# Attention with a transformed, normalised channel mixing on one core: where exponentials, first conversions and mixing steps are issued

## The chip, the cores and the metric

One core of a Trainium2 chip. The metric is the device time of one execution in microseconds (us), here the median of three runs. TensorE does the matrix products, VectorE, ScalarE and GpSimd (POOL in the rows) the elementwise work, and SyncE (SP) issues most DMA transfers. Every engine works through its own instructions in the order in which the program issues them to it.

## The reference

There are 4 batches of 8 heads; the sequence is 1152 long, a head 64 wide. Queries are averaged in pairs, so 576 remain.

```python
q_pool = q.reshape(B, H, S // 2, 2, D).mean(axis=3)
scores = np.matmul(q_pool, k.transpose(0, 1, 3, 2)) / np.sqrt(D)
attn = np.exp(scores - np.max(scores, axis=-1, keepdims=True))
attn = attn / (np.sum(attn, axis=-1, keepdims=True) + 1e-09)
x = merge_heads(np.matmul(attn, v))                      # (4, 576, 512)
u = x + np.real(np.fft.fft(np.fft.fft(x, axis=1), axis=2))
un = (u - mean(u)) / np.sqrt(var(u) + 1e-06)
out = u + np.maximum(un @ w_ch1, 0.0) @ w_ch2            # 512 -> 2048 -> 512
```

The weights `w_ch1` and `w_ch2` are in double precision.

## The kernel before

**Attention** goes over 16 pairs of heads (four per batch) and five units per pair. Units 0 to 3 hold 128 queries of each of the two heads (two tiles), unit 4 the last 64 of both (one tile). The generator `attention()` (line 290) writes out the order of the work by hand, and each `yield` hands the planner the TensorE time, in ns, of what it has just issued. In unit i these stand in turn: two score pieces of the next unit (`some(2)`), the value product of the unit before (`finish`, `av`, line 241: 36 matmuls, and a ScalarE copy, line 252), transposes of the first four key chunks (`tr`, `t_step`, line 225) with their copy from PSUM to SBUF (line 235), two score pieces, the second transposes, the exponentials of tiles that have all their three pieces (`exps()`), two score pieces, the last three groups of transposes (the second of them copied by VectorE), and the exponentials that are left.

A score piece (`s_piece`, line 197) is two matmuls of 384 keys and a VectorE eviction that keeps the running minimum (line 210). An exponential (`s_exp`, line 216) is one ScalarE operation over the tile's 1152 keys, with a read of its sum.

**PSUM** has eight tiles of one bank: five in `ps_t`, for score pieces and, from pair 4 on, for transposes; one for value products; two in `ps_f`, for transposes of pairs 0 to 3, for the transforms and the mixing. While attention goes on, the mixing uses the two of `ps_f` only.

**Heads.** Two float32r parts, high and low, stand in for one float32 factor. For heads 0 and 1 the loads come in pieces, and `k_part` and `q_part` (lines 153 to 165) convert them on ScalarE and VectorE, each piece right before the score piece that needs it; head 1's pieces follow head 0's exponential (lines 304 to 310). The loads of head 2 wait for the last exponential issued so far (`later`, line 136). Later heads are loaded in units 0 and 2 of the pair before and converted in units 1 and 3, on GpSimd and ScalarE.

**Weights.** `convert(f, which)` (line 531) turns one block of 512 KB of doubles into two float32r parts: a load (buffer `wraw`, two of them), three ScalarE operations (540, 546, 555), four VectorE operations (542 to 551), three GpSimd operations (556 to 558), a store to DRAM (561). The buffers between are single. There are 32 blocks.

**Transforms and norm.** After the last pair of a batch, `mid(b)` (line 663) issues the Fourier products and the normalisation in some fifty steps, each with its TensorE time and a due time for the next one; many of these are `gap`, 1300 ns (lines 405 and 469), 0 in the last batch.

**Channel mixing.** `ffn(b)` (line 597) has 64 steps of 12 matmuls, planned at 1600 ns each. For a step of the first product, ScalarE takes the relu from PSUM (line 611) and VectorE the low part (line 612). In batch 0 a block waits in the plan until the one two places on has been converted and stored (line 639).

**The planner** (lines 671 to 751) keeps a clock `now`, in ns of TensorE work issued, and a `credit`. After each `yield` of attention:

```python
now += pe
credit = min(credit + pe * RATE, 4000.0)
if now >= cdue and todo and len(busy) < 2:
    converter()
    cdue = now + 9000
```

It then issues what is due: a transform step where its due time has come, else mixing steps while `credit` is over 0; both are taken off `credit`. Ahead of pairs 10, 12 and 14 (`finish`, line 385) the attention outputs need a buffer of an earlier batch, and `drain` issues mixing steps, whatever the credit, until that batch is through (60 of 64 steps of batch 0, all of it, 60 of batch 1). What is left after attention is the tail.

Of the kernel before, what the change touches and what calls it, by code (L numbers as in the profile page):

```python
# [20 lines left out]
B, H, S, D = 4, 8, 1152, 64  # L21
# [25 lines left out]
def fused_kernel(ctx: ExitStack, tc: tile.TileContext, k2, q2, v2, w1, w2, cst, out):  # L47
    nc = tc.nc
    pool = lambda name, bufs, **kw: ctx.enter_context(tc.tile_pool(name=name, bufs=bufs, **kw))
    ctx.enter_context(tc.manual_schedule())  # L50
    RATE = 0.88
    XB = 5
# [163 lines left out]
    def s_exp(n, j):  # L216
        pr = n // 2
        if pr not in den:
# [4 lines left out]
                                           accum_out=den[pr][:, col:col + 1]).ins  # L223

    def t_step(pr, items, eng):

        if pr < 4:
            ps = ps_f.tile([P, 512], F32, tag="f", name="f")
        else:
            ps = ps_t.tile([P, 512], F32, tag="t", name="t")  # L230
# [59 lines left out]
    def attention():  # L290
# [12 lines left out]
        units = [(pr, j) for pr in range(NP) for j in range(5)]  # L303
        for n, (_, q_part, _, k_part, _) in enumerate(first):
            for pc in range(3):
                k_part(*K0[pc])
                if pc == 0:
                    q_part(*Q0[0])
                s_piece(n, 0, pc)
            s_exp(n, 0)  # L310
        nc.sync.dma_start(onesm, cst[4, :, P:2 * P])
# [5 lines left out]
        for i, (pr, j) in enumerate(units):  # L317
# [40 lines left out]
            if j < 4:  # L358
                a, b = tiles
# [12 lines left out]
            yield tr(g[1], "a")  # L372
            exps()
            yield some(2)
# [23 lines left out]
    def dft(b):  # L398
# [5 lines left out]
        last = smp.tile([1, SQ], F32, tag="last", name="last", bufs=1)  # L404
        gap = 1300 if b < B - 1 else 0
        nc.vector.tensor_copy(tmp[D:D + 1], ub[:1])
# [60 lines left out]
    def norm(b):  # L467
        ua, ub = ut[b]
        gap = 1300 if b < B - 1 else 0
        sm = mtile([P, 2, SQ], F32, "lsum")  # L470
# [57 lines left out]

    wsc = {}

    def convert(f, which):
        src = (w1, w2)[which]
        w = cvp.tile([P, 512, 2], I32, tag="wraw", name="wraw", bufs=2)
        nc.sync.dma_start(w, src[f].bitcast(I32).rearrange("p (c x) -> p c x", x=2))
        yield 6000
        high, low = w[:, :, 1], w[:, :, 0]
        t = cvp.tile([P, 2, 512], F32, tag="wt", name="wt")
# [19 lines left out]
        nc.gpsimd.tensor_tensor(t[:, 1, :], t[:, 1, :], hi.bitcast(F32), op=ALU.subtract)  # L557
        nc.gpsimd.tensor_tensor(lo.bitcast(F32R), t[:, 1, :], rest, op=ALU.add)  # L558
        yield 4000
        d = scw.tile([P, 2, 512], F32, name=f"w{which}_{f}")  # L560
# [110 lines left out]
    now = due = credit = 0.0  # L671
    cdue = 24000.0
    events = []
# [63 lines left out]
    for pe in attention():  # L737
        now += pe
        credit = min(credit + pe * RATE, 4000.0)
        if now >= cdue and todo and len(busy) < 2:  # L740
            converter()
            cdue = now + 9000
        run_events()
# [69 lines left out]
```

## Time and profile before

| | us |
|---|---|
| median of 3 runs | 1145.65 |
| lowest, highest | 1144.2, 1150.67 |
| the profiled execution, its own time | 1142.13 |
| its span, first to last instruction | 1140.4 |
| TensorE, VectorE, ScalarE, GpSimd busy in it | 1038.2, 603.5, 524.8, 361.9 |
| mean granted TensorE clock, share of 2.4 GHz | 0.961 |

Times in the rows count from the start of the span. Matmuls are pipelined, so the durations of single ones overlap, and the busy time of a group of them says less than the starts of one and the next.

### The profile page before, as it was taken

Reading aid. Unit: us, or ns where it says so; the run is one execution under the profiler, and the core shown is the slowest. Engines: PE = TensorE matmul, PEld = TensorE weight load, DVE = VectorE, ACT = ScalarE, POOL = GpSimd, SP = SyncE. Lnnn points to the kernel's source line nnn. Section 1 sums busy time; section 2 is a strip of 40 time slices with the busy share of each in tenths; the row PEclk is TensorE's granted clock in tenths of the full one; section 3 lists DMA queues with packets and bytes.
Section 4 is the critical chain, followed back from the end, with each engine's and each line's share of the span. In section 5 each row is a group of like instructions: output and inputs, shape, how many; then the busy total and the mean of one; then the engine's idle time right before and its main releaser. Section 6 shows DMA issues by size and latency. Waiting matters only on the chain.

```text
span 1140.4 us, 21940 instructions
## 1 busy us (share of the span) xinstructions
PE 1038.2 (91%) x8688; PEld 947.2 (83%) x8688; DVE 603.5 (53%) x1550; ACT 524.8 (46%) x1045; POOL 361.9 (32%) x343
## 2 busy tenths in 40 slices
PE   4888887897899898999999999999999899998998
PEld 2777776776788897799988998899989879998998
DVE  4476575867666557664463455744265244242222
ACT  3676675655765454564453445545156212121111
POOL 0446565675464544643222223222020010000000
PEclk9998898898899898989999999999999999998999
DMA  5644554633465756264534443335520423544554
GB/s 155 191 134 154 168 160 155 209 124 111 148 217 170 240 193 223 75 207 135 178 108 148 139 147 98 92 119 163 184 70 22 151 74 104 163 153 158 167 167 152
DMA packets 53708, 168.96 MB, mean 148 GB/s; under 512 B 8083, under 2 KB 11300, under 8 KB 53606
## 3 DMA queue, kind: packets, MB, share of 16 engines
q1 hardware_dynamic: 49286, 149.87, 41.1%
q0 software_dynamic: 4320, 17.70, 5.0%
q8 instruction: 68, 1.11, 0.4%
q14 instruction: 34, 0.28, 0.1%
HBM read 145.97 MB, written 21.57 MB: 147 GB/s over the span
## 4 chain that ended last, share of the span: by engine, by line
PE 68%; DVE 9%; POOL 6%; ACT 5%; DMA 5%; issue 5%; SPq 1%; POOLq 0%; DVEq 0%; ACTq 0%
PE o L248 12%; PE s L208 9%; PE f L593 7%; PE f L595 7%; PE f L594 7%; PE t L232 6%; PE t L593 4%; PE t L595 4%; PE t L594 4%; DVE sp L210 4%; DMA w<-wraw 2%; POOL wraw L558 2%; POOL wt L557 2%; PE f L232 2%; DMA w<-w 1%
## 5 line engine op out<-in xcount | busy, mean ns | idle before, releaser
L210 DVE TENSOR_SCALAR_CACHE_REDUCE sp<-s,bia 128x384 f32<-128x384 f32 x288 | 177.2, 615 | 87.7 <-PE s L208 67.8
L208 PE MATMUL s<-ks,qh 128*128 128x384 f32 x480 | 189.3, 394 | 37.4 <-ACT qh L156 11.4
L222 ACT ACTIVATE sp<-sp,bia 128x1152 f32<-128x1152 f32 x144 | 181.7, 1261 | 23.2 <-DVE sp L210 22.9
L248 PE MATMUL o<-pt,vs 128*64 128x128 f32 (+1 forms) x2880 | 182.2, 280 | 8.3 <-ACT pt L235 7.0
L248 PEld LDWEIGHTS o<-pt,vs 128*64 128x64 f32 x2880 | 160.1, 146 | 33.9 <-issue 21.0
L208 PE MATMUL s<-ks,ql 128*128 128x384 f32 x480 | 166.9, 348 | 0.0
L235 ACT COPY pt<-t 128x512 f32<-128x512 f32 (+2 forms) x228 | 116.3, 522 | 75.9 <-PE t L232 74.1
L232 PE MATMUL t<-ident,sp 128*128 128x128 f32 x972 | 141.4, 279 | 3.6 <-DVE sp L210 3.3
L208 PEld LDWEIGHTS s<-ks,qh 128*128 128x128 f32 x480 | 94.1, 196 | 49.2 <-DVE sp L210 14.9
L232 PEld LDWEIGHTS t<-ident,sp 128*128 128x128 f32 x972 | 116.8, 143 | 14.8 <-DVE sp L210 5.4
L593 PE MATMUL f<-unh,w 128*128 128x288 f32 x332 | 102.3, 308 | 5.5 <-DMA w<-w 5.5
L593 PE MATMUL f<-g,w 128*128 128x288 f32 x336 | 103.1, 307 | 1.6 <-DMA w<-w 1.6
L612 DVE SCALAR_TENSOR_TENSOR g<-f,g 128x288 fp32r<-128x288 f32 x83 | 38.0, 457 | 117.5 <-ACT g L611 117.5
L595 PE MATMUL f<-g,w 128*128 128x288 f32 x336 | 99.5, 296 | 0.0
L594 PE MATMUL f<-g,w 128*128 128x288 f32 x336 | 99.4, 296 | 0.0
L594 PE MATMUL f<-unh,w 128*128 128x288 f32 x332 | 99.1, 298 | 0.0
L595 PE MATMUL f<-unl,w 128*128 128x288 f32 x332 | 98.8, 298 | 0.0
L208 PEld LDWEIGHTS s<-ks,ql 128*128 128x128 f32 x480 | 94.9, 198 | 0.7 <-DVE ql L157 0.3
L623 DVE TENSOR_TENSOR x<-f,x 128x288 f32<-128x288 f32 x84 | 38.4, 457 | 103.8 <-PE f L595 103.7
L556 POOL TENSOR_TENSOR rest<-rest,wt 128x512 f32<-128x512 f32 x32 | 43.6, 1361 | 143.8 <-DVE wt L551 138.3
L178 POOL TENSOR_TENSOR ks<-kr,ks 64x1152 fp32r<-64x1152 f32 x30 | 79.6, 2653 | 27.5 <-issue 18.0
L210 DVE TENSOR_SCALAR_CACHE_REDUCE sp<-s 128x384 f32<-128x384 f32 x144 | 78.6, 546 | 14.3 <-PE s L208 11.0
(132 smaller groups left out, 2030.7 us busy)
## 6 DMA issues: line engine op xcount, KB each, us to landing
w<-w SPq DMA_DIRECT2D x128, 512.0 KB
ks<-in_k POOLq DMA_DIRECT2D x30, 576.0 KB, 5.2
qr<-in_q SPq DMA_DIRECT2D x30, 576.0 KB
wraw<-in_w SPq DMA_DIRECT2D x32, 512.0 KB
w<-wraw SPq DMA_DIRECT2D x32, 512.0 KB
vs<-in_v SPq DMA_DIRECT2D x32, 288.0 KB
kr<-in_k SPq DMA_DIRECT2D x30, 288.0 KB
out<-x SPq DMA_DIRECT2D x12, 288.0 KB
```

What stands on the lines that cost most here:

```text
L178: nc.gpsimd.tensor_tensor(ks[D:, :], kr[D:, :], ks[D:, :].bitcast(F32), op=ALU.subtract)
L208: nc.tensor.matmul(ps, lhsT=l, rhs=k, start=i == 0, stop=i == len(ops) - 1)
L210: nc.vector.tensor_scalar(sp[n, j][:, c], ps, -0.0625, bt[:, pc - 1:pc] if pc else None, op0=ALU.mult, op1=ALU.min, accum_out=bt[:, pc:pc ...
L222: last_exp[0] = nc.scalar.activation(t, t, AF.Exp, bias=bia.pop((n, j))[:, 2:3], scale=-1.0, accum_out=den[pr][:, col:col + 1]).ins
L232: nc.tensor.transpose(ps[:, i * P:i * P + P], sp[k][:, c * P:(c + 1) * P], ident)
L235: (nc.vector.tensor_copy if eng == "v" else nc.scalar.copy)(pt[:, :o], ps[:, :o])
L248: nc.tensor.matmul(po[y * D:y * D + D, :w], lhsT=qkv[2 * pr + y][3][:, c, :], rhs=pt[:, o:o + w], start=c == 0, stop=c == NKC - 1)
L556: nc.gpsimd.tensor_tensor(rest, rest, t[:, 0, :], op=ALU.mult)
L593: nc.tensor.matmul(ps, lhsT=ah, rhs=bh, start=first, stop=False)
L594: nc.tensor.matmul(ps, lhsT=al, rhs=bh, start=False, stop=False)
L595: nc.tensor.matmul(ps, lhsT=ah, rhs=bl, start=False, stop=last)
L623: nc.vector.tensor_tensor(x[:, c], ps[:, :HT], x[:, c], op=ALU.add)
```

## The change

Six edits. `RATE`, the mixing credit per TensorE time of attention, goes from 0.88 to 1.05. In pairs 0 to 3 every fifth group of transposes (counted over all of them, five in units 0 to 3 and three in unit 4) takes its PSUM tile from `ps_t` and not from `ps_f`. The parts of heads 0 and 1 are converted ahead of the score pieces of the head before: all of head 0's parts, then head 1's in between head 0's three score pieces, then head 0's exponential, head 1's three pieces and its exponential. The exponentials in the middle of a unit are left to its end. `gap` goes from 1300 to 600 ns. The first conversion starts at 60000 and not at 24000 ns of the planner's clock, then one follows each 10000 ns until the first mixing is queued and each 8500 ns from then on (9000 before), and a conversion between its first ScalarE and its last GpSimd operation keeps another from beginning that part.

```diff
@@ -48,7 +48,7 @@
     nc = tc.nc
     pool = lambda name, bufs, **kw: ctx.enter_context(tc.tile_pool(name=name, bufs=bufs, **kw))
     ctx.enter_context(tc.manual_schedule())
-    RATE = 0.88
+    RATE = 1.05
     XB = 5
     cp = pool("const", 1)
     kv = pool("kv", 4)
@@ -222,9 +222,12 @@
         last_exp[0] = nc.scalar.activation(t, t, AF.Exp, bias=bia.pop((n, j))[:, 2:3], scale=-1.0,
                                            accum_out=den[pr][:, col:col + 1]).ins
 
+    steps = [0]
+
     def t_step(pr, items, eng):
 
-        if pr < 4:
+        steps[0] += 1
+        if pr < 4 and steps[0] % 5 != 2:
             ps = ps_f.tile([P, 512], F32, tag="f", name="f")
         else:
             ps = ps_t.tile([P, 512], F32, tag="t", name="t")
@@ -301,13 +304,21 @@
             v_load()
             q_load(*Q0[2])
         units = [(pr, j) for pr in range(NP) for j in range(5)]
-        for n, (_, q_part, _, k_part, _) in enumerate(first):
-            for pc in range(3):
-                k_part(*K0[pc])
-                if pc == 0:
-                    q_part(*Q0[0])
-                s_piece(n, 0, pc)
-            s_exp(n, 0)
+        def parts(n):
+            _, q_part, _, k_part, _ = first[n]
+            k_part(*K0[0])
+            yield q_part(*Q0[0])
+            yield k_part(*K0[1])
+            yield k_part(*K0[2])
+
+        for _ in parts(0):
+            pass
+        for pc, _ in enumerate(parts(1)):
+            s_piece(0, 0, pc)
+        s_exp(0, 0)
+        for pc in range(3):
+            s_piece(1, 0, pc)
+        s_exp(1, 0)
         nc.sync.dma_start(onesm, cst[4, :, P:2 * P])
         for _, q_part, _, _, _ in first:
             for c in Q0[1:]:
@@ -370,7 +381,6 @@
             yield tr(g[0], "a")
             yield some(2)
             yield tr(g[1], "a")
-            exps()
             yield some(2)
             for y, x in enumerate(g[2:]):
                 yield tr(x, "v" if j < 4 and y == 1 else "a")
@@ -402,7 +412,7 @@
 
         tmp = mtile([P, 2, SQ], F32, "tmp")
         last = smp.tile([1, SQ], F32, tag="last", name="last", bufs=1)
-        gap = 1300 if b < B - 1 else 0
+        gap = 600 if b < B - 1 else 0
         nc.vector.tensor_copy(tmp[D:D + 1], ub[:1])
         nc.scalar.copy(last, ub[D:D + 1, 1, :])
         yield 0, gap
@@ -466,7 +476,7 @@
 
     def norm(b):
         ua, ub = ut[b]
-        gap = 1300 if b < B - 1 else 0
+        gap = 600 if b < B - 1 else 0
         sm = mtile([P, 2, SQ], F32, "lsum")
         for j in range(2):
             nc.vector.tensor_tensor(sm[:, j], ua[:, j], ub[:, j], op=ALU.add)
@@ -527,12 +537,16 @@
 
 
     wsc = {}
+    inside = []
 
     def convert(f, which):
         src = (w1, w2)[which]
         w = cvp.tile([P, 512, 2], I32, tag="wraw", name="wraw", bufs=2)
         nc.sync.dma_start(w, src[f].bitcast(I32).rearrange("p (c x) -> p c x", x=2))
         yield 6000
+        while inside:
+            yield 400
+        inside.append(f)
         high, low = w[:, :, 1], w[:, :, 0]
         t = cvp.tile([P, 2, 512], F32, tag="wt", name="wt")
         a, b = t[:, 0, :].bitcast(I32), t[:, 1, :].bitcast(I32)
@@ -556,6 +570,7 @@
         nc.gpsimd.tensor_tensor(rest, rest, t[:, 0, :], op=ALU.mult)
         nc.gpsimd.tensor_tensor(t[:, 1, :], t[:, 1, :], hi.bitcast(F32), op=ALU.subtract)
         nc.gpsimd.tensor_tensor(lo.bitcast(F32R), t[:, 1, :], rest, op=ALU.add)
+        inside.pop()
         yield 4000
         d = scw.tile([P, 2, 512], F32, name=f"w{which}_{f}")
         nc.sync.dma_start(d, h.bitcast(F32))
@@ -669,7 +684,7 @@
         ready.append(b)
 
     now = due = credit = 0.0
-    cdue = 24000.0
+    cdue = 60000.0
     events = []
     tick = itertools.count()
     ready = []
@@ -739,7 +754,7 @@
         credit = min(credit + pe * RATE, 4000.0)
         if now >= cdue and todo and len(busy) < 2:
             converter()
-            cdue = now + 9000
+            cdue = now + (10000 if nb == 0 else 8500)
         run_events()
         while nb < B and nb < len(started):
             fills.append(ffn(nb))
```

## Rows read from the trace of the kernel before

**Rows 1.** This is the page's table of engines: busy us (share of the span) and instructions, over the whole span.

```profile
PE 1038.2 (91%) x8688; PEld 947.2 (83%) x8688; DVE 603.5 (53%) x1550; ACT 524.8 (46%) x1045; POOL 361.9 (32%) x343
```

**Rows 2.** This is the busy time of each engine in each stretch (stretch in us from the span's start, its length, busy us and instructions of PE, PEld, DVE, ACT, POOL, then the mean granted TensorE clock, the DMA share and GB/s). The cuts lie where ScalarE copies out the first value product of pairs 0, 1, 2, 3, 4, 6 and 10; then at 798.4 and 827.0, between which there is channel mixing only; at the last value product (899.3); and at 1038.4.

```profile
0.00:33.25 33.25, 15.55 (x83) 11.46 (x84) 16.17 (x47) 13.18 (x25) 3.85 (x13) 1.00 0.49 146
33.25:69.10 35.85, 31.14 (x323) 27.43 (x324) 21.57 (x64) 24.28 (x48) 15.65 (x15) 1.00 0.54 171
69.10:112.60 43.50, 35.47 (x323) 30.85 (x324) 28.29 (x72) 27.68 (x55) 25.72 (x23) 0.88 0.52 162
112.60:156.90 44.30, 36.12 (x323) 31.52 (x324) 26.83 (x72) 27.80 (x55) 25.44 (x23) 0.88 0.50 159
156.90:201.00 44.10, 36.24 (x323) 31.51 (x324) 26.99 (x71) 27.82 (x56) 25.11 (x23) 0.88 0.52 160
201.00:308.40 107.40, 93.18 (x761) 77.14 (x761) 78.11 (x191) 67.89 (x131) 60.51 (x56) 0.90 0.47 149
308.40:577.10 268.70, 252.02 (x2124) 229.84 (x2125) 158.62 (x406) 141.31 (x281) 131.15 (x117) 0.96 0.57 181
577.10:798.40 221.30, 215.71 (x1916) 198.33 (x1914) 120.10 (x332) 114.97 (x227) 59.07 (x60) 0.99 0.41 125
798.40:827.00 28.60, 28.60 (x218) 28.60 (x217) 8.24 (x18) 3.29 (x8) 2.14 (x4) 1.00 0.56 182
827.00:899.30 72.30, 67.35 (x680) 61.06 (x678) 39.13 (x106) 39.73 (x80) 7.56 (x5) 0.98 0.21 68
899.30:1038.40 139.10, 128.18 (x889) 121.10 (x890) 50.60 (x110) 24.35 (x52) 5.68 (x8) 0.96 0.39 129
1038.40:1140.40 102.00, 98.62 (x743) 98.39 (x741) 28.84 (x63) 12.53 (x31) 0.00 (x0) 1.00 0.50 162
```

**Rows 3.** This is the startup in order of time, VectorE, ScalarE and TensorE (start us, duration us, engine, line, operation, tiles, shapes; in brackets the idle time before it and what ended it).

```profile
3.70 0.56 DVE L165 TENSOR_TENSOR ks<-kr,ks 64x384 fp32r<-64x384 f32 x1 [3.70 <-ACT ks L164]
...
6.24 0.56 DVE L210 TENSOR_SCALAR_CACHE_REDUCE sp<-s 128x384 f32<-128x384 f32 x1 [0.78 <-PE s L208]
...
6.83 0.56 DVE L165 TENSOR_TENSOR ks<-kr,ks 64x384 fp32r<-64x384 f32 x1
...
11.46 1.25 ACT L222 ACTIVATE sp<-sp,bia 128x1152 f32<-128x1152 f32 x1 [5.38 <-DVE sp L210]
...
12.72 0.49 ACT L164 CAST ks<-kr 128x384 fp32r<-128x384 f32 x1
...
20.79 1.25 ACT L222 ACTIVATE sp<-sp,bia 128x1152 f32<-128x1152 f32 x1 [5.51 <-DVE sp L210]
...
22.59 0.69 PE L208 MATMUL s<-ks,qh 128*128 128x384 f32 x1 [2.50 <-ACT qh L156]
```

**Rows 4.** This is TensorE in unit 1 of pair 0, in order of time, same columns.

```profile
35.47 1.03 PE L232 MATMUL f<-ident,sp 128*128 128x128 f32 x8
37.39 0.44 PE L232 MATMUL f<-ident,sp 128*128 128x128 f32 x2 [0.88 <-ACT pt L235]
37.58 0.43 PE L208 MATMUL s<-ks,qh 128*128 128x384 f32 x1
...
38.47 2.19 PE L248 MATMUL o<-pt,vs 128*64 128x128 f32 x36
```

**Rows 5.** This is ScalarE in the same unit, in order of time, same columns.

```profile
35.51 1.26 ACT L222 ACTIVATE sp<-sp,bia 128x1152 f32<-128x1152 f32 x1
36.66 0.19 ACT L222 ACTIVATION_READ_ACCUMULATOR sp<-sp,bia 128x1 f32 x1
36.76 0.58 ACT L235 COPY pt<-f 128x512 f32<-128x512 f32 x1
37.86 0.37 ACT L235 COPY pt<-f 128x256 f32<-128x256 f32 x1 [0.53 <-PE f L232]
```

**Rows 6.** This is the chain of work that ended last, in pair 2 (start us, us, what).

```profile
119.08 7.92 DMA w<-wraw
...
127.07 3.89 DMA wraw<-in_w
...
131.04 0.07 ACT wt L540
...
131.60 0.58 ACT pt L235
...
132.23 1.67 PE f L232 x8
```

**Rows 7.** This is line 548, a conversion's VectorE operation, over the span (count: shortest, median and longest in ns, first and last start us).

```profile
L548 DVE SCALAR_TENSOR_TENSOR wt<-wraw,wt x32: 671/687/2720, 65.6 to 507.7; 128x512 int32<-128x512 int32 x32
```

**Rows 8.** This is line 540, a conversion's first ScalarE operation, over the span (same columns), and what its engine waited for ahead of it (us, times).

```profile
L540 ACT ACTIVATE wt<-wraw x32: 647/665/707, 61.0 to 498.0; 128x512 f32<-128x512 f32 x32
...
  POOL wraw L558: 34.7, 17
```

**Rows 9.** This is SyncE's queue, what its transfers waited for (us in total, times, longest).

```profile
SPq L534 <- DMA w<-wraw: 126.3, 29, 10.2
```

**Rows 10.** This is the chain of work that ended last, weight loads in the tail (start us, us, what).

```profile
1019.67 4.20 DMA w<-w
...
1028.38 4.26 DMA w<-w
```

## The prediction, made before the changed kernel was run

> **What bounds the kernel now.** I read the engine table first, then the span cut at the first value product of each pair, then single units and the chain of waits. TensorE is busy 1038.2 of 1140.4 us [rows 1], so the stalls to be won sum to 102 us; the rest is work that the change doesn't touch. The cut [rows 2] shows where they lie: 17.7 us before the first value product (33.25 - 15.55), 29.0 in pairs 0 to 3, 14.2 in pairs 4 and 5, 16.7 in pairs 6 to 9, 10.5 in pairs 10 to 15 and 14.3 after attention. The same rows show the granted clock: 1.00 in pair 0, 0.88 in pairs 1 to 3, 0.90 in pairs 4 and 5, 0.96 to 1.00 later. Where stalls stand, the clock is low too, so a stall removed can be worth more than its length.
>
> Three things make these stalls. **Startup**: head 1's key conversion starts at 12.72, behind head 0's exponential (11.46); on VectorE each conversion after the first (3.70) stands behind an eviction (6.24 before 6.83). The second exponential starts at 20.79 and the next score matmul at 22.59 [rows 3]. **The unit's own wait**: in a unit without conversion, TensorE waits 0.88 us before the last two transposes, for a ScalarE copy [rows 4]; ScalarE shows why, its third copy (36.76) stands behind the exponential of 35.51 [rows 5]. **Weight conversion**: pair 0, with only the start of one at its end, takes 35.9 us, pairs 1 to 3, with three each by the plan below, 43.5, 44.3 and 44.1 [rows 2], so one costs (44.2 - 35.9)/3 = 2.8 us there. The chain goes through it: store 7.92 us, load of the next raw weights 3.89, then the copies of the unit behind it in ScalarE's queue, then the transposes [rows 6].
>
> **The planner, before and after.** Which work lies beside which follows from lines 679 to 751, gone through with their own costs. A unit is worth 6 x 390 + 18 x 105 + 1950 = 6180 ns, a pair 28.9 us; its credit rises from 25.4 to 30.3 us, 3.1 mixing steps of 1.6 us more per pair. This order fits the trace: it has a drain of 20 steps ahead of unit 14.0, and there 28.6 us hold nothing but mixing, 218 matmuls, which at 12 a step are 18 steps of 1.57 us [rows 2]. For the changed kernel it gives: channel mixing of batch 0 starts some 14 us of planner time sooner (smaller gaps), 6 steps fall into unit 6.0 and before where there were none; 60 steps are done ahead of pair 10 in both; at attention's end 157 instead of 130; and the drain ahead of pair 14 is gone. Conversions: 6 instead of 10 ahead of pair 4, 13 instead of 17 ahead of 6.0, 19 instead of 15 in pairs 6 to 9. They are shifted, not thinned: on average 10.4 us of planner time lie between two before, 11.3 after. Two never overlap between their first ScalarE operation and their last GpSimd one in either plan, so the new lock costs nothing; if real lag made it matter, it would only delay a conversion.
>
> **The terms.** Against the profiled execution, 1142.1 us (span 1140.4); the median of the runs is 1145.7, 3.5 above.
>
> 1. Startup. Both heads' conversions run ahead of the evictions. From 3.70 on VectorE then has six key subtractions (0.56), four short query operations (some 0.3 each) and head 0's three evictions (0.62 and a read of 0.08): 6.6 us, with some 1.2 us of waits for ScalarE's copies 11.5, where the first exponential starts now too. Head 1's three evictions follow directly, 2.1 us: second exponential at 13.6 instead of 20.79 [rows 3]. All loads keep their order in SP's queue. The next score matmul, head 2's loads, which wait for that exponential, and all behind them move with it: **-7** (bounds -5 to -8; if a load of head 1 is late, it is by 1 to 2 us).
>
> 2. Both exponentials at the end, in pairs 0 to 3. ScalarE then has 2 x 1.45 = 2.9 us of them in one piece [rows 5], while TensorE has two pieces (0.8) and the value product (2.1) to do [rows 4]: 2.9 too. The next unit's first transposes need only the first exponential, so they are covered by some 0.9 us. After that ScalarE is late with its copies by 0.3 + 0.6, and the last transposes of a unit, whose PSUM tile is freed by the third copy, still wait about 0.5 us where the rotation puts none of the last four groups into the larger pool (pairs 0 and 2), nothing where it does (pairs 1 and 3). The tile that a transpose takes from the larger pool leaves four to the score pieces, whose evictions of 0.6 us keep up; no cost. So 4 x 0.4 and 4 x 0.88 per pair: 10.2 over four pairs; I halve it in pairs 2 and 3, where conversions may end last: **-8** (0 to -14). Copies that come sooner need no cover; the exponentials' cover is the value product.
>
> Here a rule speaks against the exponentials as the cause. The 0.88 us comes back in unit after unit. The Trainium skill (Perfetto Trace Analysis, "Optimization Strategy") says that the same gap repeating can mean too few PSUM buffers. By that the term would be the rotation's alone, 4 x 0.88 in the two pairs where it moves one of the last groups, -7. The trace agrees in part: the wait is for a PSUM tile, but the copy that frees it is late because of the exponential.
>
> 3. Conversions paced anew. Pair 1 loses its three: 43.5 becomes 35.9, **-8**. Four come back in pairs 6 to 9. The price there: 268.7 us less 228 of planned work [rows 2], less 20 x 0.24 because a value product takes 2.19 us [rows 4] and is planned at 1.95, over 15: 2.4 us each, **+10** (0 to +11, 4 x 2.8). The pacing itself is worth nothing; what differs is which neighbours the stalls have.
>
> 4. Smaller gaps: 6 steps, 9.6 us of mixing, move from pairs 6 to 9 into pairs 4 and 5, which have 14.2 us idle at a clock of 0.90 [rows 2]. I take **-7** (0 to -9.6). VectorE operations of the transforms come closer together: at 78.1 of 107.4 us busy there it has room.
>
> 5. More mixing per unit: 27 steps move from the tail into pairs 10 to 15. TensorE's work is the same; won is only the idle time that they fill. Units 10.1 to 10.3 and 14.1 to 15.2 had no mixing: of 10.5 us idle in these pairs 4.9 lie in the stretch 827.0 to 899.3, 5.6 ahead of 798.4, where pair 10 is a sixth of it [rows 2]. I take **-6** (0 to -10). In pairs 4 to 9 the mixing of batch 0 now catches up with the conversions, which then set its pace; each load follows its own store closely, a new wait in SP's queue, ahead of raw loads and heads. SP waits there already for such stores, 126.3 us in 29 waits [rows 9], so I take **+1** (0 to +10).
>
> 6. The tail: 43 us shorter as pairs 10 to 15 get longer, net nothing. Its waits stay: 14.3 us idle, of which two weight loads on the chain take 4.20 and 4.26 [rows 10]. The last transform has 10 us of planned mixing between its sums and its last products instead of 53: **+2** (0 to +8).
>
> 7. Exponentials in the 60 units from pair 4 on: transposes there use five tiles, TensorE often has mixing to do. **-7** (0 to -15), 0.12 us a unit: between nothing and pair 0's 0.88, nearer to nothing, since idle is rare in these rows [rows 2].
>
> Sum: -7 - 8 - 8 + 10 - 7 - 6 + 1 + 2 - 7 = -30: 1142 becomes **1112**.
>
> **Rivals.** (A) Conversions decide everywhere: the chain of store, raw load and ScalarE queue [rows 6] with ScalarE waiting 34.7 us for GpSimd [rows 8] ends last in all pairs that convert, so terms 2, 4 and 7 vanish but for pair 0 (-2), term 3 is -8 + 11, and the new wait of term 5 is +4: -7 - 2 + 3 - 6 + 4 + 2 = -6, 1136; half so, 1124. For it: 32 conversions start between 61.0 and 498.0 us, 14 us apart [rows 8]. Against: pair 1's own gain needs no faster loop.
> (B) The clock returns: without the repeated wait, pairs 0 to 3 and 4, 5 stay at 1.00 as pair 0 does. At 0.88, a quarter of 132 us ran at 1.2 instead of 2.4 GHz, which cost 16 us, at 0.90 of 107 us 11 us; half of these 27, and half of the 14 us that terms 2 and 7 leave to their bounds: 1112 - 14 - 7 = 1091.
> (C) Slower: the pair of exponentials blocks the mixing. A step's PSUM tile is freed by a ScalarE operation behind them; TensorE has two such tiles, and 50 units from pair 6 on carry three steps each. If in each the second exponential (1.45) were waited for: 73 us against the 30 won, 1185; it decides from 30/50 = 0.6 us a unit. Against it: between the exponentials' issue and the second step behind them stand a value product and two pieces, 2.9 us; steps come one by one as credit comes in. The Trainium skill (Perfetto Trace Analysis, "Tensor Engine Instruction") calls ScalarE a strict first-in first-out engine, as the copy behind the exponential shows here [rows 5]; by that the wait is possible, not its length.
> (D) The conversions get dearer where they go: an operation of 0.69 us took up to 2.72 beside GpSimd work [rows 7]. The transforms' GpSimd adds fall into the same pairs. All 32 at 1 us more, 32 us against 30: 1144, no change.
>
> **Chances.** Forecast 0.56; A 0.17; B 0.14; C 0.06; D 0.07. A measurement tells about 0.5% (6 us) here: faster, below 1140, has the forecast, A and B: 0.87; same 0.07; slower 0.06. Range: the sum of the bounds taken as independent is some 15 us either way, 1097 to 1127; to hold 8 in 10 it takes in A to its half and most of it beyond, and B: 1085 to 1136.
>
> **What would show it.** Second exponential near 13.6, next score matmul near 15.5; pair 0 about 34, pair 1 like pair 0, pairs 2 and 3 near 42; no wait of 0.9 in front of the last transposes; unit 14.0 without a stretch of pure mixing; attention's end near 915 and a tail near 198 us. Wrong it is if relu operations wait behind two exponentials with TensorE idle, if conversions lie more than 15 us apart, or if TensorE waits for weights in pairs 7 to 9.

## The result, and the profile after

The changed kernel takes 1116.0 us (four runs, 1109.4 to 1118.4) where the kernel before takes 1146.4 (four runs too, one more than in the table ahead): 30.3 us less, a ratio of 0.972 [0.967, 0.977]. The forecast was 1112, -30. The total was right and several of its terms were not: too small a gain in pairs 0 to 3 and an unforeseen loss, most of it ahead of pair 10, made up for each other. The profiled execution took 1109.4, the lowest of the four, so its stretches together show 32.8.

The engine table: TensorE's idle time fell from 102 to 82 us [rows 1]. The other 12.8 of the 32.8 us are busy time, with the same 8688 matmuls; the mean granted clock rose from 0.961 to 0.967.

```profile
PE 1025.4 (93%) x8688; PEld 946.0 (85%) x8688; DVE 605.9 (55%) x1550; ACT 527.9 (48%) x1045; POOL 363.5 (33%) x343
```

The span cut at the same places as in [rows 2], without the cuts inside the last six pairs: startup, pairs 0, 1, 2, 3, then 4 and 5, 6 to 9, 10 to 15, and the tail in two parts (columns as there).

```profile
0.00:26.18 26.18, 16.43 (x83) 12.40 (x84) 15.97 (x47) 13.25 (x25) 4.58 (x13) 1.00 0.61 186
26.18:57.68 31.50, 30.57 (x323) 27.50 (x324) 18.55 (x60) 23.18 (x47) 13.72 (x14) 1.00 0.53 161
57.68:88.18 30.50, 30.21 (x323) 27.52 (x324) 18.46 (x60) 23.19 (x47) 14.04 (x14) 1.00 0.47 145
88.18:124.29 36.11, 31.46 (x323) 27.77 (x324) 28.92 (x71) 27.43 (x55) 22.87 (x21) 1.00 0.55 176
124.29:160.16 35.87, 33.31 (x323) 30.39 (x324) 24.51 (x72) 27.24 (x54) 22.00 (x22) 0.91 0.58 177
160.16:275.07 114.91, 100.37 (x833) 86.75 (x834) 88.79 (x203) 73.56 (x142) 68.45 (x59) 0.94 0.52 165
275.07:546.92 271.85, 248.41 (x2104) 226.49 (x2105) 178.07 (x428) 146.27 (x286) 143.57 (x127) 0.96 0.57 186
546.92:905.31 358.39, 347.35 (x3080) 327.85 (x3079) 165.78 (x465) 162.33 (x326) 68.59 (x68) 0.98 0.39 125
905.31:1005.60 100.29, 88.67 (x565) 80.97 (x566) 38.05 (x83) 18.90 (x38) 5.66 (x8) 0.91 0.33 110
1005.60:1107.60 102.00, 98.62 (x743) 98.39 (x741) 28.80 (x63) 12.52 (x31) 0.00 (x0) 1.00 0.49 162
```

In one table, with the kernels of the experiments below; each time is that between two cuts. Each row is one execution. Executions of the same code differ too: pairs 10 to 15 and the tail, which are the same in before, rotation_alone and pacing_alone, take 563.3 to 567.1 us together, so a difference of 4 us there shows nothing.

| us | startup | pair 0 | 1 | 2 | 3 | 4, 5 | 6 to 9 | 10 to 15 | tail | span |
|---|---|---|---|---|---|---|---|---|---|---|
| before | 33.2 | 35.9 | 43.5 | 44.3 | 44.0 | 107.4 | 268.7 | 322.2 | 241.1 | 1140.4 |
| changed | 26.2 | 31.5 | 30.5 | 36.1 | 35.9 | 114.9 | 271.8 | 358.4 | 202.3 | 1107.6 |
| exps_alone | 33.1 | 33.1 | 43.3 | 41.9 | 40.1 | 108.6 | 263.1 | 321.5 | 244.1 | 1128.9 |
| rotation_alone | 33.0 | 34.2 | 42.6 | 45.4 | 42.8 | 106.5 | 268.8 | 322.8 | 243.8 | 1140.0 |
| pacing_alone | 33.1 | 36.0 | 36.2 | 38.0 | 38.0 | 117.9 | 279.3 | 322.8 | 244.3 | 1145.6 |
| exps_rotation | 32.4 | 33.0 | 42.8 | 41.5 | 43.2 | 107.1 | 264.3 | 319.5 | 244.0 | 1127.7 |
| after_mid_exps | 26.2 | 33.1 | 33.7 | 37.3 | 38.3 | 113.5 | 271.3 | 359.8 | 199.4 | 1112.6 |
| after_old_pacing | 25.7 | 32.4 | 43.0 | 41.9 | 41.2 | 118.5 | 272.2 | 357.4 | 180.4 | 1112.7 |
| after_low_rate | 25.9 | 31.5 | 30.5 | 35.0 | 36.6 | 113.8 | 255.2 | 328.0 | 231.3 | 1087.8 |
| after_old_gap | 26.2 | 31.5 | 30.5 | 35.9 | 36.8 | 117.1 | 266.0 | 365.5 | 198.8 | 1108.2 |
| rate_late | 26.0 | 31.5 | 30.5 | 35.3 | 36.6 | 114.1 | 258.8 | 362.9 | 204.4 | 1100.1 |
| earlier_conversions | 25.3 | 31.5 | 30.5 | 36.5 | 35.3 | 120.9 | 275.3 | 356.5 | 180.4 | 1092.3 |

Where the 32.8 us come from: startup -7.1, pairs 0 to 3 -33.7, pairs 4 to 9 +10.6, pairs 10 to 15 and the tail together -2.6.

**Startup**, ScalarE and TensorE in order of time, to be held against [rows 3]:

```profile
8.26 0.92 ACT L164 CAST ks<-kr 128x384 fp32r<-128x384 f32 x2
...
11.68 1.25 ACT L222 ACTIVATE sp<-sp,bia 128x1152 f32<-128x1152 f32 x1 [2.49 <-DVE sp L210]
...
13.65 1.25 ACT L222 ACTIVATE sp<-sp,bia 128x1152 f32<-128x1152 f32 x1 [0.62 <-DVE sp L210]
...
15.45 0.69 PE L208 MATMUL s<-ks,qh 128*128 128x384 f32 x1 [3.40 <-ACT qh L156]
```

Head 1's key conversions (8.26) no longer stand behind an exponential, the second exponential starts at 13.65 (forecast 13.6, before 20.79) and the next score matmul at 15.45 (forecast 15.5, before 22.59).

**The unit's own wait**, TensorE in unit 1 of pair 0, as [rows 4]:

```profile
28.41 1.03 PE L235 MATMUL f<-ident,sp 128*128 128x128 f32 x8
29.73 0.44 PE L235 MATMUL f<-ident,sp 128*128 128x128 f32 x2 [0.29 <-ACT pt L238]
```

ScalarE in the same unit, as [rows 5]:

```profile
29.09 0.58 ACT L238 COPY pt<-f 128x512 f32<-128x512 f32 x1 [0.55 <-PE f L235]
30.21 0.37 ACT L238 COPY pt<-f 128x256 f32<-128x256 f32 x1 [0.53 <-PE f L235]
30.48 1.26 ACT L222 ACTIVATE sp<-sp,bia 128x1152 f32<-128x1152 f32 x1
31.63 0.19 ACT L222 ACTIVATION_READ_ACCUMULATOR sp<-sp,bia 128x1 f32 x1
31.73 1.24 ACT L222 ACTIVATE sp<-sp,bia 128x1152 f32<-128x1152 f32 x1
```

The third copy (29.09) has no exponential ahead of it, the wait of 0.88 us is 0.29, and both exponentials follow at the end.

**What is new.** SyncE's queue, as [rows 9]; line 545 loads raw weights, 601 loads a converted block for the mixing:

```profile
SPq L545 <- DMA w<-wraw: 57.9, 22, 8.0
...
SPq L601 <- DMA w<-wraw: 31.3, 8, 7.5
```

The raw loads wait for half as long as before (57.9 instead of 126.3 us), but the mixing's loads now wait for the store of their own block, 31.3 us in eight waits. TensorE hardly feels them: none of its waits of more than 0.25 us in pairs 6 to 9 is for a weight load. What it mostly waits for is VectorE. Just ahead of pair 10, at the end of batch 0's mixing, the chain of work that ended last reads:

```profile
526.80 2.52 DVE unl L532
...
530.88 1.16 DVE wt L558
...
532.04 0.38 DVE x L638
...
532.46 0.61 PE f L608
...
533.07 0.24 PE f L609
```

and TensorE there, with the idle time ahead of it (the bracket):

```profile
532.46 0.61 PE L608 MATMUL f<-g,w 128*128 128x288 f32 x1 [5.02 <-DVE x L638]
```

A mixing step waits 5.02 us because VectorE reaches its eviction (line 638) late, behind a norm operation of 2.52 us (line 532, otherwise 0.75) and a conversion's (line 558). After it the matmuls are 0.24 us apart, not 0.13: the granted clock is that of 1.2 GHz from 530.4 to 537.2, and the mean of 518.0 to 546.9 is 0.88.

### The profile page after: what moved, and what is told of

Its sections match the earlier page's. It is cut to its first block, busy times and chain, and to the rows that moved or that the text cites. A ratio compares the mean times of both kernels' runs of the same rounds, so it can differ in the third digit from the quotient of the medians.

```text
span 1107.6 us, 22010 instructions
## 1 busy us (share of the span) xinstructions
PE 1025.4 (93%) x8688; PEld 946.0 (85%) x8688; DVE 605.9 (55%) x1550; ACT 527.9 (48%) x1045; POOL 363.5 (33%) x343
## 4 chain that ended last, share of the span: by engine, by line
PE 72%; DVE 12%; ACT 4%; DMA 4%; POOL 4%; issue 3%; SPq 1%; POOLq 0%; DVEq 0%; ACTq 0%
PE s L208 11%; PE o L251 11%; PE f L608 8%; PE t L235 8%; PE f L609 7%; PE f L610 7%; DVE sp L210 3%; PE t L608 3%; PE t L610 3%; PE t L609 3%; PE f L235 2%; PE f L451 2%; DMA w<-w 2%; PE f L459 2%; ACT sp L222 1%
## 5 line engine op out<-in xcount | busy, mean ns | idle before, releaser
L238 ACT COPY pt<-t 128x512 f32<-128x512 f32 (+2 forms) x243 | 125.4, 526 | 123.3 <-PE t L235 119.6
L251 PE MATMUL o<-pt,vs 128*64 128x128 f32 (+1 forms) x2880 | 168.0, 270 | 12.3 <-DVE pt L238 9.4
L251 PEld LDWEIGHTS o<-pt,vs 128*64 128x64 f32 x2880 | 147.6, 140 | 34.8 <-issue 19.0
L235 PE MATMUL t<-ident,sp 128*128 128x128 f32 x1045 | 152.7, 278 | 4.3 <-ACT sp L222 2.8
L235 PEld LDWEIGHTS t<-ident,sp 128*128 128x128 f32 x1045 | 126.2, 143 | 13.7 <-ACT sp L222 3.4
L608 PE MATMUL f<-unh,w 128*128 128x288 f32 x376 | 117.1, 312 | 9.1 <-DMA w<-w 8.4
L627 DVE SCALAR_TENSOR_TENSOR g<-f,g 128x288 fp32r<-128x288 f32 x94 | 42.9, 456 | 146.4 <-ACT g L626 146.4
L608 PE MATMUL f<-g,w 128*128 128x288 f32 x360 | 111.2, 309 | 5.0 <-DVE x L638 5.0
L609 PE MATMUL f<-unh,w 128*128 128x288 f32 x376 | 112.9, 300 | 0.0
L610 PE MATMUL f<-unl,w 128*128 128x288 f32 x376 | 112.7, 300 | 0.0
L609 PE MATMUL f<-g,w 128*128 128x288 f32 x360 | 107.0, 297 | 0.0
L610 PE MATMUL f<-g,w 128*128 128x288 f32 x360 | 107.0, 297 | 0.0
L626 ACT ACTIVATE g<-f 128x288 fp32r<-128x288 f32 x94 | 38.3, 409 | 116.7 <-PE f L610 116.3
```

The costliest lines, as they stand in the source:

```text
L235: nc.tensor.transpose(ps[:, i * P:i * P + P], sp[k][:, c * P:(c + 1) * P], ident)
L238: (nc.vector.tensor_copy if eng == "v" else nc.scalar.copy)(pt[:, :o], ps[:, :o])
L251: nc.tensor.matmul(po[y * D:y * D + D, :w], lhsT=qkv[2 * pr + y][3][:, c, :], rhs=pt[:, o:o + w], start=c == 0, stop=c == NKC - 1)
L608: nc.tensor.matmul(ps, lhsT=ah, rhs=bh, start=first, stop=False)
L609: nc.tensor.matmul(ps, lhsT=al, rhs=bh, start=False, stop=False)
L610: nc.tensor.matmul(ps, lhsT=ah, rhs=bl, start=False, stop=last)
```

## The experiments

All were compared with runs of the kernel before on the same chip; times below are medians, ratios are to the kernel before.

**1. The exponentials alone**, and **2. the rotation alone**, both on the kernel before:

```diff
             yield tr(g[1], "a")
-            exps()
             yield some(2)
```

> The kernel before with the exponentials in the middle of a unit left to its end, nothing else. Theory (the exponential ahead of the third copy makes the wait): the wait of 0.88 us before the last transposes falls to 0.3 to 0.5, pair 0 from 35.9 to 33 or 34, pairs 1 to 3 from 44 to 40 or 41, the run 1146 to about 1131. Rival 1 (too few PSUM tiles make the wait): pair 0 stays at 35.9, the run at 1146. Rival 2 (the move also cheapens the conversions, because their ScalarE operations no longer meet an exponential in the middle of a unit): pairs 1 to 3 at 38 or less, the run at 1125 or less.

```diff
+    steps = [0]
...
-        if pr < 4:
+        steps[0] += 1
+        if pr < 4 and steps[0] % 5 != 2:
             ps = ps_f.tile([P, 512], F32, tag="f", name="f")
```

> The kernel before with every fifth group of transposes of pairs 0 to 3 in the larger PSUM pool, nothing else. Theory: pairs 0 and 2 unchanged, pairs 1 and 3 lose part of their waits, the run at 1140 to 1146. Rival (the number of PSUM tiles is the cause of the unit's wait): the wait goes in every unit where the rotation moves one of the last groups, pairs 1 and 3 shorter by 4 us each, the run near 1138.

The exponentials alone gave 1129.5, 0.988 [0.982, 0.993]; the rotation 1138.9, 0.998 [0.995, 1.001], no measurable difference. The same transposes of the same unit tell why, first with the exponentials moved:

```profile
36.61 0.44 PE L232 MATMUL f<-ident,sp 128*128 128x128 f32 x2 [0.29 <-ACT pt L235]
```

then with the rotation:

```profile
37.18 0.44 PE L235 MATMUL f<-ident,sp 128*128 128x128 f32 x2 [0.88 <-ACT pt L238]
```

0.29 against an unchanged 0.88. So moving the exponential away from ahead of the copy takes most of the wait, as the theory had it. The unchanged 0.88 tells nothing of the rotation, though: these rows are from pair 0, where it moves only the second of the five groups, and the tile that the last transposes need is the same as before. In pairs 1 and 3 it moves the fourth and the third. There the last transposes wait no more in any unit of pair 1, and at most 0.39 us in pair 3; unit 1 of pair 1, where the kernel before waits 2.54 us at this place, with the value product behind it (a row without a bracket has no wait):

```profile
70.37 0.38 PE L235 MATMUL f<-ident,sp 128*128 128x128 f32 x2
...
73.22 2.18 PE L251 MATMUL o<-pt,vs 128*64 128x128 f32 x34 [1.41 <-ACT pt L238]
```

The Trainium skill (Perfetto Trace Analysis, "Optimization Strategy") says that a gap that repeats can mean too few PSUM buffers; the trace agrees in pair 1, where another tile for one group ends the wait. So the wait needs both, a late copy and a tile that is wanted again at once, and either edit removes all or most of it. Rival 1 is right about the waits of pairs 1 and 3 and wrong about the price: they come down by 0.9 and 1.3 us, not 4. Part of the wait goes to the value product (1.41 above), part to a unit with a conversion (in unit 3 of pair 1, 3.63 us ahead of the third group instead of 0.35). Rival 2 fails: with the exponentials alone pairs 1 to 3 come down by 0.2, 2.4 and 3.9 only.

**3. The pacing alone**, on the kernel before:

```diff
-    cdue = 24000.0
+    cdue = 60000.0
...
+        while inside:
+            yield 400
+        inside.append(f)
...
+        inside.pop()
...
-            cdue = now + 9000
+            cdue = now + (10000 if nb == 0 else 8500)
```

> The kernel before with the conversions' new start, their new spacing and the lock, nothing else. Theory: pair 1 falls from 43.5 to 36, pairs 2 and 3 stay at 44, pairs 6 to 9 get 8 to 10 us longer, the run stays within 1142 to 1150. Rival (the new pacing is what made the conversions of pairs 2 and 3 cheap): pairs 2 and 3 near 38 to 40, the run near 1130.

1145.1, 1.001 [0.998, 1.004]. Pairs 1, 2, 3, then 4 and 5, then 6 to 9:

```profile
69.11:105.27 36.16, 31.03 (x323) 27.41 (x324) 20.56 (x60) 23.08 (x46) 14.01 (x14) 1.00 0.40 122
105.27:143.26 37.99, 31.71 (x323) 27.69 (x324) 29.11 (x71) 27.13 (x54) 22.80 (x21) 1.00 0.50 156
143.26:181.30 38.04, 33.00 (x323) 29.01 (x324) 24.09 (x72) 27.01 (x54) 22.05 (x22) 0.96 0.58 183
181.30:299.16 117.86, 99.37 (x761) 80.35 (x762) 81.04 (x191) 68.34 (x131) 63.48 (x57) 0.87 0.45 142
299.16:578.49 279.33, 256.94 (x2129) 233.26 (x2130) 170.77 (x423) 147.52 (x293) 147.71 (x129) 0.95 0.59 190
```

The net is what the theory said, its parts are not. Pairs 2 and 3 still begin three conversions each, and take 38 us instead of 44: the rival is right about the price there. But 10.4 us come back in pairs 4 and 5, which hold seven conversions in both kernels, and 10.6 in pairs 6 to 9, which hold four more. Where the conversions lie against the units changes their price.

**4. Exponentials and rotation together**, both edits on the kernel before.

> The kernel before with the exponentials at the unit's end and the rotation of the transposes' tiles, nothing else. If the two add up: the sum of what each gives alone, near 1128. If one needs the other (without the exponential in between, a third tile is what the last transposes still lack): pair 0 near 31.5 as in the changed kernel, the run under 1126. If they do the same work twice: no better than the better one of the two.

1128.9, 0.989 [0.985, 0.993], pair 0 at 33.0: no better than the exponentials alone. In the changed kernel pair 0 takes 31.5, and there no conversion begins at its end any more.

**5. The changed kernel with the exponentials in the middle again** (the line of experiment 1 put back).

> The changed kernel with the exponentials of full tiles in the middle of a unit again. Alone, their move gave 14.6 us. If it gives as much here: 1116 becomes 1131, pairs 0 and 1 back to 34 to 36 each. If mixing and the new pacing already cover part of the wait: 1122 to 1126. If the move costs something behind pair 6 (relus behind two exponentials), pairs 6 to 15 come out shorter here than in the changed kernel.

1116.9, 0.975 [0.971, 0.979]: not to be told from the changed kernel. In its trace pairs 0 to 3 are 8.4 us longer, as term 2 had it, and all that follows 3.5 us shorter, which is within the differences between executions; the whole run tells 0.9 us only. So term 7 is not there. Pairs 10 to 15 and the tail together are 559.1 against 560.7 us, nothing like the 73 us of rival (C): it is out.

The trace also shows what the rotation does without a conversion near. In pair 0 the last transposes of a unit wait 0.88 us again, and its first four value products start 7.43, 8.14 and 6.71 us apart; in the changed kernel it is 6.86, 7.58 and 6.21. In pair 1, where the rotation moves the fourth group, no transposes wait (unit 1 below), and the value products start 6.35, 7.07 and 5.73 us apart, in the changed kernel 6.35, 7.06 and 5.72. In these units the rotation alone does as much as both edits.

```profile
68.84 0.38 PE L235 MATMUL f<-ident,sp 128*128 128x128 f32 x2
```

**6. The changed kernel with the old pacing, 7. with the old credit, 8. with the old gap:**

```diff
-    cdue = 60000.0
+    cdue = 24000.0
...
-            cdue = now + (10000 if nb == 0 else 8500)
+            cdue = now + 9000
```

> The changed kernel with conversions from 24000 ns on and each 9000 ns. Pacing alone moved 20 us out of pairs 1 to 3 and 21 us into pairs 4 to 9. Theory (it only moves the stalls): pairs 1 to 3 longer by some 15, pairs 4 to 9 shorter by as much, the run within 1112 to 1120. Rival (in the changed kernel the mixing fills the later stalls, so pacing and mixing work together): slower by 5 to 10, near 1124.

```diff
-    RATE = 1.05
+    RATE = 0.88
```

> The changed kernel with a mixing credit of 0.88. Theory: the tail is 35 to 40 us longer and attention's last pairs as much shorter, net 4 to 8 us slower, 1120 to 1124, with the stretch of pure mixing ahead of pair 14 back. Rival (the mixing per unit is what hides the conversions of pairs 4 to 9): 10 us or more slower, and that in pairs 4 to 9. Rival (it only moves steps): 1116.

```diff
-        gap = 600 if b < B - 1 else 0
+        gap = 1300 if b < B - 1 else 0
```

> The changed kernel with the transforms' gap of 1300 ns. Theory: 6 mixing steps fewer ahead of pair 6, pairs 4 and 5 shorter by about 7, pairs 6 to 9 longer by 10, the run 2 to 5 us slower, 1118 to 1121. Rival (no gain, since the steps only change places): 1116.

The last edit stands in two places, in the transforms and in the norm.

Old pacing: 1121.6, 0.978 [0.973, 0.982], intervals that overlap with the changed kernel's; pairs 1 to 3 are 23.5 us longer, the rest makes up for most of it: from pair 4 on 928.5 us against 947.4.

Old credit: **1096.5, 0.959 [0.955, 0.962], some 20 us faster than the changed kernel** (15 by the ratios). None of the three expectations had that. Of the 19.8 us between the two profiled executions, 16.7 lie in pairs 6 to 9 by the cuts (255.2 against 271.8). But the cut at pair 10 is a ScalarE copy, and in the changed kernel it comes 6.8 us after the value product has ended, while TensorE works on. The start of that value product is the fairer place, with 4218 and 4219 matmuls begun by then. Up to there, in pair 9, and from there to the cut, first with the old credit:

```profile
0.00:525.11 525.11, 477.63 (x4218) 426.71 (x4218) 363.29 (x927) 333.05 (x652) 283.00 (x263) 0.97 0.57 182
466.15:525.11 58.96, 58.64 (x531) 55.69 (x530) 41.88 (x109) 39.12 (x77) 30.35 (x29) 1.00 0.64 212
525.11:528.42 3.31, 3.31 (x45) 3.11 (x45) 1.26 (x4) 0.47 (x1) 3.23 (x2) 1.00 0.33 130
```

then of the changed kernel:

```profile
0.00:537.97 537.97, 481.81 (x4219) 430.07 (x4219) 369.41 (x928) 334.12 (x652) 287.92 (x264) 0.96 0.55 176
468.56:537.97 69.41, 59.96 (x496) 54.62 (x495) 46.89 (x109) 38.52 (x76) 40.68 (x36) 0.92 0.53 174
537.97:546.92 8.95, 8.95 (x89) 8.75 (x89) 3.87 (x12) 0.00 (x0) 1.32 (x4) 1.00 0.71 218
```

So 12.9 us are lost ahead of pair 10, all of it in pair 9: 10.4 us longer for 35 matmuls fewer, with 9.5 us idle and a granted clock of 0.92. Of these 9.5 us, 8.3 end with VectorE. The other 6.9 us of the 19.8 lie behind; what they come from is not shown. By the planner's costs the changed kernel has a drain of 13 us ahead of pair 10, in which batch 0's last four steps wait for the last conversions, with no attention between; with the old credit it has 3.2 us, and no block waits for a conversion.

Old gap: 1110.2, 0.970 [0.966, 0.974], no loss. The run shows nothing of term 4, but its stretches do. Pairs 4 and 5, from value product to value product, first of the changed kernel, then with the old gap, and pair 9 with the old gap:

```profile
157.93:272.84 114.91, 100.37 (x833) 86.75 (x832) 89.07 (x206) 73.67 (x141) 66.30 (x58) 0.94 0.52 164
158.58:273.52 114.94, 97.76 (x761) 79.96 (x760) 79.00 (x191) 68.81 (x131) 63.37 (x57) 0.87 0.47 147
480.87:541.72 60.85, 60.70 (x543) 57.99 (x543) 42.72 (x107) 35.49 (x71) 29.45 (x27) 0.99 0.59 199
```

In the same time the changed kernel does 72 matmuls more, the six steps of term 4. But with the old gap the plan has no drain ahead of pair 10, and pair 9 is free of idle time: what the smaller gap wins in pairs 4 and 5 goes again in pair 9. So the drain is not the credit's alone.

**9. The higher credit only after batch 0:**

```diff
-        credit = min(credit + pe * RATE, 4000.0)
+        credit = min(credit + pe * (RATE if (0, 1) in done_f2 else 0.88), 4000.0)
```

> The changed kernel with a mixing credit of 0.88 until batch 0 is mixed (ahead of pair 10) and 1.05 from then on. Theory (the higher credit hurts only ahead of pair 10, where the mixing of batch 0 catches up with the conversions): pairs 6 to 9 at 255 as with 0.88 throughout, pairs 10 to 15 and the tail together at 556 to 561, the run near 1096. Rival (more mixing in the late units hurts as well): pairs 10 to 15 and tail over 565, the run at 1103 or more. Rival (the late mixing fills idle time, as forecast, 6 us): under 1091.

1102.9, 0.963 [0.959, 0.968]. Pairs 6 to 9 are back at 258.8, and pair 10's first value product starts at 526.8 with 4219 matmuls begun, near the old credit's 525.1: the higher credit does its harm ahead of it. Pairs 10 to 15 and the tail are 567.4, which is what the rival asked for. Counted from that value product, with 4471 matmuls left in each, the old credit takes 562.7 us, the changed kernel 569.6 and this one 573.3. So late mixing at the higher credit fills no idle time; in these executions it costs 7 to 11 us. It is not the credit alone, as the next experiment shows.

**10. The higher credit with earlier conversions:**

```diff
-    cdue = 60000.0
+    cdue = 45000.0
```

> The changed kernel, credit 1.05, with conversions from 45000 ns on instead of 60000, so that by the plan one block instead of seven waits for its conversion and no drain is left ahead of pair 10. Theory (the mixing that waits for the last conversions is what costs 16 us ahead of pair 10): pairs 1 to 3 some 8 us longer, pair 9 some 14 shorter, the run 1105 to 1112. Rival (the credit itself costs it, by steps that get in the way of attention): 1120 or more, pair 9 not shorter than the work that it holds.

**1093.7, 0.957 [0.952, 0.961]**, with the credit at 1.05 and more of a gain than expected. The waits of the mixing's loads in SyncE's queue:

```profile
SPq L601 <- DMA w<-wraw: 4.9, 2, 3.2
```

They wait for stores twice, 4.9 us, instead of eight times, 31.3. By the plan 71 steps instead of 60 are done ahead of pair 10, and there is no drain. So 17.6 us of work come sooner: pair 10's first value product starts 15.2 us later than in the changed kernel with that work done (4350 matmuls), and what is left takes 30.4 us less. Less the 17.6, 2 us are won ahead of it and 13 behind it. Ahead of it pair 9 is 8 us cheaper by its work (60 matmuls more in 69.0 us, 4.8 idle), and pairs 4 to 8 are some 7 dearer. Why so much is won behind it, with the same credit, is not shown. Pairs 1 to 3 are not some 8 us longer, as expected: they take 102.4 us against 102.5, though two conversions begin in pair 1, which takes 30.5 us as without any.

So it is not the credit that costs some 20 us but the credit together with conversions that end late: either taken back gives about the same. Experiment 6 agrees: its conversions end earlier still, its plan has no drain either, and from pair 4 on it is as short as with the old credit (928.5 and 928.4 us). Old credit and earlier conversions together were not tried.

**11 and 12. Without the conversions' arithmetic**, on either kernel: the ten operations are gone, the loads of the doubles stay, and a constant block is stored.

```diff
-        nc.scalar.activation(t[:, 0, :], high.bitcast(F32), AF.Abs)
...
-        nc.gpsimd.tensor_tensor(lo.bitcast(F32R), t[:, 1, :], rest, op=ALU.add)
...
-        nc.sync.dma_start(d, h.bitcast(F32))
+        nc.sync.dma_start(d, fixed)
```

> The kernel before without the arithmetic of the 32 conversions (their ten operations on ScalarE, VectorE and GpSimd); the loads of the doubles stay, the stores write a constant block instead. Theory (a conversion costs TensorE 2.4 to 2.8 us of stall): 77 to 90 us shorter, 1056 to 1069, pairs 1 to 3 at 36 each. Rival (they only fill waits that others would make): under 40 us shorter.

> The changed kernel without the arithmetic of the 32 conversions, in the same way. Theory (the change took a third off a conversion's price in pairs 2 and 3, but not later): 55 to 70 us shorter than the changed kernel, 1046 to 1061, pairs 2 and 3 at 31. Against the kernel before without that work: 22 us shorter if the startup (7) and the exponentials (15) are all that is left; more if the higher credit helps where no conversion is in the way; less if it hurts by itself.

1079.0, 0.944 [0.940, 0.948], and 1060.6, 0.927 [0.922, 0.932]: 66 and 55 us shorter than the kernels that they come from. The first is less than the 77 to 90 expected. Pairs 0 to 3, 4 and 5, 6 to 9 of the kernel before without them:

```profile
33.36:176.38 143.02, 124.19 (x1289) 109.63 (x1290) 81.37 (x240) 92.29 (x184) 54.58 (x55) 1.00 0.59 193
176.38:270.94 94.56, 87.58 (x761) 73.39 (x762) 64.31 (x165) 56.53 (x109) 32.95 (x35) 0.96 0.51 168
270.94:514.63 243.69, 240.07 (x2124) 223.09 (x2125) 125.65 (x342) 118.00 (x235) 65.07 (x68) 0.99 0.60 199
```

and of the changed one:

```profile
25.36:148.83 123.47, 121.36 (x1289) 109.98 (x1290) 73.92 (x240) 92.73 (x185) 56.72 (x56) 1.00 0.58 183
148.83:248.16 99.33, 95.40 (x833) 82.85 (x834) 63.56 (x173) 61.50 (x119) 34.04 (x37) 0.97 0.58 187
248.16:493.93 245.77, 239.69 (x2092) 222.16 (x2092) 126.30 (x351) 116.55 (x229) 62.77 (x67) 0.98 0.64 206
```

Against the whole kernels the arithmetic costs 24.7, 12.9 and 25.0 us before, with 10, 7 and 15 conversions (2.5, 1.8 and 1.7 us each), and 10.5, 15.6 and 26.1 after, with 6, 7 and 19 (1.8, 2.2 and 1.4). And the four pairs without conversions fall from 143.0 to 123.5 us, with the clock at 1.00 in both: that is what exponentials and rotation are worth where nothing is in their way, 19.5 us (the raw loads, which stay, also come at other times), of which conversions hide more than half in the kernel before.

The second kernel also tells what the drain costs by itself, for its plan is that of the changed kernel. Its pair 9, from value product to value product:

```profile
427.25:485.13 57.88, 56.57 (x496) 53.00 (x495) 32.93 (x89) 30.84 (x61) 18.54 (x19) 0.96 0.59 184
```

The same matmuls take 57.9 us, not 69.4, with 1.3 us idle. Its mixing's loads wait even longer for stores, 49.4 us in ten waits. So neither the drain nor those waits make the loss of pair 9 by themselves: it comes with the arithmetic of the four conversions that begin there. With the old credit four begin in pair 9 too, without a long drain, and 0.3 us are idle. It takes both.

## Why the prediction came out right, point by point

- **Term 1, startup, -7**: measured -7.1, with both starting times within 0.1 us.
- **Term 2, the exponentials in pairs 0 to 3, -8**: measured -9.2 alone and, in the stretches, -8.4 within the change. The mechanism is as told: in the changed kernel the last transposes wait some 0.3 us in pairs 0 and 2 and not at all in pair 1. The size was low: without conversions the two edits give 4.5 to 5.6 us a pair, 19.5 together, where the sum had 1.6 and 3.5, 10.2 together. What conversions hide brought it back to the forecast. The rule on PSUM buffers, set aside in the term, holds in pair 1, where the rotation alone ends the wait. (In pair 0 the rotation does move one of the last four groups, the second; but that frees nothing for the last.)
- **Term 3, pacing, -8 + 10**: measured -19.6 in pairs 1 to 3 and +21.1 in pairs 4 to 9. The net was right; the step that failed is that a conversion keeps its price wherever it is shifted to: in pairs 2 and 3 three conversions cost 8.3 us before and 1.9 with the new pacing.
- **Term 4, smaller gaps, -7**: there in pairs 4 and 5, where six steps more cost no time, and lost again in pair 9; without it the kernel is no slower.
- **Term 5, more mixing, -6 and +1**: the term that failed most. The place was named, batch 0's mixing catching up with the conversions, but not the wait: it was priced as loads behind their own stores in SyncE's queue, at +1, at most +10. What TensorE waits for in pair 9 is VectorE, with a norm's and the conversions' operations in its queue. The same plan showed the 13 us of drain, which I read as "60 steps done in both". The credit there costs some 20 us, 12.9 of them ahead of pair 10. The 6 us of filled idle time are not there: from pair 10's first value product on, the higher credit takes 569.6 us and the old one 562.7.
- **Term 6, the tail**: 202.3 us against a forecast of 198, the weight loads' waits unchanged in kind.
- **Term 7, later exponentials, -7**: alone, pairs 6 to 9 fell by 5.6 and pairs 4 and 5 rose by 1.2; within the change nothing.
- **"The rest is work that the change doesn't touch"**: 12.8 of the 32.8 us came out of TensorE's busy time, which the sum counted as fixed. (In the rows the idle time of pairs 0 to 3 is 28.8 us, not 29.0; nothing hangs on it.)

So the sum was held up by two errors, which is luck: pairs 0 to 3 gained 33.7 us where terms 2 and 3 gave 16, and the credit lost some 20 where term 5 gave a gain of 5. Of the rivals, (A) and (D) put the conversions' cost where they go, which is true of pairs 4 to 9 (+21 alone); (B) is true of pairs 0 to 2, whose clock is 1.00 in the changed kernel, but 0.91 to 0.96 from pair 3 to pair 9 took its place; (C) is refuted.

What stays open: why a conversion's price in pairs 2 and 3 falls to a quarter with the same three per pair (start and spacing were changed together; the lock had nothing to hold back, for in the trace before no conversion starts ahead of the last GpSimd operation of the one before; experiment 10, with another start and the new spacing, keeps the price low, so the start of 60000 is not needed for it); and why the changed kernel and experiment 9 are dearer behind pair 10 than experiments 8 and 10.

## What to carry to other kernels

When a plan lets a consumer run faster, go through the plan for the place where it catches up with its producer, and price the whole stretch, with the producer's work on every engine that the consumer needs there, not the single wait. Try such a rate with the producer's start as a second knob: here either one alone was worth some 20 us more than the pair that was chosen. Edits that move stalls must be read by stretches, since a net of nothing (experiment 3) held 20 us each way. And stretches must end where the same work has been done: a cut that waits for something itself moved 4 us of experiment 8 from one side to the other.

## What the runs showed of the hardware

A stall can cost more than its length: after the wait of 5.02 us the mixing's matmuls ran 0.24 us apart for some 5 us and 0.13 from then on, the granted clock's two levels. And VectorE's subtraction of the norm (line 532), some 0.75 us in twelve of its sixteen runs, took up to 2.60. First its durations over the span (count: shortest, median, longest in ns), then GpSimd's operation beside the longest one, which ran from 526.73 to 529.33:

```profile
L532 DVE TENSOR_TENSOR unl<-d,unh x16: 748/753/2596, 245.9 to 984.4; 128x576 fp32r<-128x576 f32 x16
```

```profile
525.67 3.04 POOL L178 TENSOR_TENSOR ks<-kr,ks 64x1152 fp32r<-64x1152 f32 x1
```

The GpSimd operation ends at 528.71, and VectorE's 0.62 us behind it. The four longer ones, 0.87 to 2.60 us, all overlap GpSimd operations on tensors; of the twelve others one does. Line 548 showed the same before [rows 7]: its longest, 2.72 us at 107.0, overlaps GpSimd's line 178 by 2.17 us. The Trainium skill (GPSIMD Engine Reference, "8. Key points") says that GpSimd shares its SBUF interfaces with VectorE and gets in the way of instructions with two SBUF inputs; the trace agrees, by a factor of 3.5 here.
